# Hash attention and a PReLU block on one core: opening copies shared with VectorE, w_out's sums one step earlier, another way out for the last two blocks

## The chip, the cores and the metric

The kernel runs on one core of a Trainium2 chip. Its time is the device time of one execution in microseconds, as the median of several runs; smaller is better. Names of engines in the views: PE is TensorE (PEld its weight loads), DVE VectorE, ACT ScalarE, POOL GpSimd, SP SyncE, which here only issues DMAs.

## What is computed

The reference, cut to what matters:

```python
# attention: batch 4, heads 8, sequence 768, head size 64; proj is 64 x 6
q_bits = einsum(q, proj) > 0;  k_bits = einsum(k, proj) > 0     # 6 bits each
mask = bucket(q_bits) == bucket(k_bits)
scores = where(mask, (q @ k.T) / sqrt(64), -1e9)
attn = softmax(scores) @ v
x = attn as (3072 tokens, 512)
# feed-forward: w_in 512 x 2048, w_out 2048 x 512, alpha 2048
h = x @ w_in
g = maximum(h, 0) + alpha * minimum(h, 0)
out = g @ w_out
```

The two weights arrive as 64-bit floats; the kernel makes 32-bit floats of them on the core itself, and both weight products are done with seven instead of eight block products (Strassen), which needs sums of blocks of x, w_in, g and w_out.

## The kernel before

**Two paths.** `fast_path` does all the work under the assumption that the magnitudes are moderate; its `verdict` writes a flag, and only if that flag is set does `general_path` run behind it. In the runs here the fast path is what is timed. Most instructions are recorded with `do`, which keeps each engine's order as it is written in the program. DMAs are not recorded with it, so a scheduler may place them otherwise on SP's and POOL's queues.

**Attention** goes over 16 pairs of heads, each in two units of 384 queries (u = 0 to 31). `load` fetches q, k and v of a pair. `turn` transposes q and k on PE into a score bank pair and copies them out (qT, kT). `hash_bits` multiplies both with proj and turns the signs into bits (qb, kb). `scores` makes, for each of six blocks of keys, the products of the bits and of q and k in one bank pair (`sc`), and ACT takes the exponential into `pt`. The row sums are added beside it: `add_first` (L748) adds blocks 0 and 1 on DVE and has POOL issue a DMA that adds block 2 into the same tile (accp, L749); `add_last` adds blocks 3 to 5 (accd); `add_total` (L757) adds both. `attend` (L767) multiplies with v into the bank `av`, `totals` (L779) sums accd over the keys on PE into the bank `sm`, and `divide` normalizes and writes x (L808), from where it is stored.

PSUM has eight banks: three pairs that go around under tag "sc" (scores, transposes, hash banks, the "a" banks of the products), one "av", one "sm". So attend(u + 1) may start only when x of unit u has read `av`, and a score block only when the third one before it in that pool has been read.

**Weights** are converted in 32 pieces beside attention, one for each unit: `weight_abs` (ACT), `weight_clamp`, `weight_parts` and `weight_sum` (DVE). Piece 0 and the abs and clamp of piece 1 lie before or in unit 0.

**Opening.** Half of pair 0 is turned and hashed with DVE's help (`turn(..., DVE)`, `hash_bits(..., DVE)`), the other half and pair 1 by ACT alone. With `engine` DVE, hash_bits has a bank of its own for q's hashes (hsq, in `sm`), so that ACT and DVE can read different banks.

**Feed-forward.** For each of four batches come eight blocks "1" (`ff1`, products f_0 to f_7) and seven blocks "2" (`ff2`, products z_1 to z_7, in the order 1, 2, 5, 6, 3, 7, 4); j counts all blocks. `Product.step` issues parts of a product on PE: it uses the banks a (a pair of "sc"), b (`sm`) and c (`av`); `keep` copies a bank to SBUF with ACT, and `finish` adds the four quarters (named 11, 12, 21, 22) on DVE. In ff2, `finish` writes acc; for z_4 it adds the tile of z_1 (m1) too.

w_out's sums are formed once, in blocks j = 1 to 6 of the first batch: `load_out(n)` reads part n of eight on POOL's queue into the tile wo (two parts a tile, tag "wl", two buffers), `sum_out(n)` does four adds on DVE (L944) and stores the part on POOL's queue (L945). From j = 6 on `load_w2` loads whole w_out tiles on SP's queue (L928) into the same two buffers of tag "wl"; the first takes the memory of wo4 (parts 4 and 5), the second that of wo6 (parts 6 and 7), so each waits until those parts are stored. `largest` and `verdict` stand at j = 4.

**Output.** Results leave by `turn_out`: DVE transposes and twelve small DMAs on SP's queue (L1016). The last two blocks use `turn_last` (PE transposes, ACT copies at L1037, DMAs at L1038): block o_5 first, before the last part of z_4; then block o_4, which is z_4 itself. The tile of o_5 has tag "o" (two buffers, shared with turn_out), that of o_4 tag "m5" (one buffer).

Of the kernel before, what the change touches and what calls it, by code (L numbers as in the profile page):

```python
# [8 lines left out]
F32 = mybir.dt.float32  # L9
# [397 lines left out]
def fast_path(  # L407
# [165 lines left out]

    def weight_abs(i):
        i = order[i]
        lo, hi = halves(i)
        wx[i] = pool.tile([P, 512], F32, name=f"wx{i}", tag="wx")
        do(ACT.activation(wx[i], hi.bitcast(F32), AF.Abs))  # L580

    def weight_clamp(i):
# [105 lines left out]
    def hash_bits(pi, halves=BOTH, engine=None):  # L688

        if halves.start == 0:
            bits["q", pi] = qbs[pi % 2]
            bits["k", pi] = pool.tile([P, S], BF16, name=f"kb{pi}", tag="kb")
        ps = {"k": two_banks(f"hs{pi}")}
        ps["q"] = psum.tile([P, 1, 512], F32, name=f"hsq{pi}", tag="sm") if engine is DVE else ps["k"]
        for half in range(halves.start, halves.stop):
            for n, name in enumerate("kq"):
                for s in range(2):
                    r, c = D * s, D * (s ^ half) + 32 * n  # L700

                    for t, c in [("k", c)] + ([("q", c ^ D)] if engine is DVE and name == "q" else []):
                        do(PE.matmul(
                            ps[t][c : c + 32, half, :CW], wh[r : r + D],
                            tr[name, pi][r : r + D, half * CW : (half + 1) * CW], start=True, stop=True,
                        ))
        for half in range(halves.start, halves.stop):
            cols = slice(half * CW, (half + 1) * CW)
            for s in range(2):
                c = D * (s ^ half ^ (engine is DVE)) + 32  # L710
                do(ACT.activation(  # L711
                    bits["q", pi][D * s : D * s + 32, cols], ps["q"][c : c + 32, half, :CW], AF.Sign, bias=hb[c : c + 32],
                ))

            for to, c, n in [(0, 0, P)] if half == 0 else [(0, D, D), (D, 0, D)]:
                dst, src = bits["k", pi][to : to + n, cols], ps["k"][c : c + n, half, :CW]
                if engine is DVE:
                    do(DVE.tensor_scalar(
                        dst, src, hb_k[c : c + n, 0:1], hb_k[c : c + n, 1:2], op0=ALU.is_gt, op1=ALU.subtract,
                    ))  # L720
                else:
                    do(ACT.activation(dst, src, AF.Sign, bias=hb[c : c + n]))  # L722
# [112 lines left out]
    class Product:  # L835

        def __init__(self, name, width, nk, left, right, finish):
            self.name, self.width, self.nk = name, width, nk  # L840
            self.left, self.right, self.finish = left, right, finish
            self.ps, self.sb = {}, {}

# [20 lines left out]
        def step(self, n):  # L864
            if n == 1:
                self.times("a", 0, 0, True)
                self.keep("a", "p1")
            elif n == 2:
                self.times("b", 1, 1, True)
            elif n == 22:  # L870
                self.finish("11", self.sb["p1"], self.ps["b"])
            elif n == 5:
                self.times("c", 3, 3, True)
                self.keep("c", "p5")
            elif n == 6:
                self.times("a", 4, 4, False)
                self.keep("a", "u1")
            elif n == 3:
# [91 lines left out]
    def ff2(b, n):  # L970
# [11 lines left out]
        def finish(c, x, more):  # L982
            i, jj = int(c[0]) - 1, int(c[1]) - 1
            dst = acc[:, i, jj * HC : (jj + 1) * HC]
            if more is not None:
                do(DVE.tensor_tensor(dst, x, more, op=ALU.add))
                if p == 4:
                    add(4, 1, i, jj)
            elif p == 4:
                do(DVE.tensor_tensor(dst, x, m2[b, 1][:, i, jj * HC : (jj + 1) * HC], op=ALU.add))  # L990
            else:
                do(ACT.copy(dst, x))
            if c == "21":

                for to, x in {2: [(2, 1)], 6: [(1, 6)], 3: [(3, 5), (3, 1)], 7: [(1, 7), (5, 1)]}.get(p, []):
                    add(to, x)
                done = {2: (2, 0, 0), 3: (3, 0, 1), 7: (5, 1, 1), 4: (4, 1, 0)}.get(p)
                if done:
                    to_turn.append((b, *done))

        return Product(
            f"z{b}_{p}", HC, HK, lambda m, k: w2[b, n, m][:, k], lambda m, k: g2[b, n, m][:, k], finish,
        )

    def turn_out():
# [14 lines left out]

    def turn_last(n):

        b, p, half, ch = to_turn.pop(0)
        o = late[0].tile([P, CH, P, 2], F32, name=f"o_{p}", tag=("o", "m5")[n], bufs=2 - n)
        dst = out_v[b, ch * CH : (ch + 1) * CH].rearrange("c p d -> p c d")[:, :, half * 2 * P : (half + 1) * 2 * P]
        goes = [([(t, i) for i in range(2) for t in range(CH)], slice(0, CH))]
        if n:
            goes = [([(2, 0), (2, 1), (0, 0), (1, 0)], slice(2, CH)), ([(0, 1), (1, 1)], slice(0, 2))]
        for cells, ts in goes:
            ps = two_banks(f"to{p}").rearrange("p a f -> p (a f)").rearrange("p (i t f) -> p i t f", i=2, f=P)  # L1030
            for t, i in cells:
                do(PE.transpose(ps[:, i, t], m2[b, p][:, i, t * P : (t + 1) * P], ident))
            for i in range(2):
                t = [c[0] for c in cells if c[1] == i]
                if t:
                    t = slice(min(t), max(t) + 1)
                    do(ACT.copy(o[:, t, :, i], ps[:, i, t]))  # L1037
            (nc.scalar if n else nc.sync).dma_start(dst[:, ts], o[:, ts].rearrange("p t f i -> p t (f i)"))  # L1038


    top = const.tile([P, 4], F32, name="top")
    row = const.tile([1, 4], F32, name="row")

    def largest():
        do(DVE.tensor_reduce(top[:, :2], mags, axis=mybir.AxisListType.X, op=ALU.max))
        do(DVE.tensor_reduce(top[:, 2:3], wmax, axis=mybir.AxisListType.X, op=ALU.max))
        do(DVE.tensor_reduce(top[:, 3:4], alpha, axis=mybir.AxisListType.X, op=ALU.max))

    def verdict():
        ps = psum.tile([1, 4, P], F32, name="vd", tag="sm")  # L1050
        for n in range(4):
            do(PE.transpose(ps[:, n], top[:, n : n + 1], ident))
        do(DVE.tensor_reduce(row, ps, axis=mybir.AxisListType.X, op=ALU.max))
        do(DVE.tensor_tensor(row[:, 0:1], row[:, 0:1], row[:, 1:2], op=ALU.mult))

        do(DVE.tensor_scalar(row[:, 0:1], row[:, 0:1], SAFE, None, op0=ALU.is_le))
        do(DVE.tensor_scalar(row[:, 2:3], row[:, 2:3], HI_END, None, op0=ALU.is_lt))
        do(DVE.tensor_scalar(row[:, 3:4], row[:, 3:4], 1.0, None, op0=ALU.is_le))
        do(DVE.tensor_tensor(row[:, 0:1], row[:, 0:1], row[:, 2:3], op=ALU.mult))
        do(DVE.tensor_tensor(row[:, 0:1], row[:, 0:1], row[:, 3:4], op=ALU.mult))  # L1060
        do(DVE.tensor_scalar(flag, row[:, 0:1], -1.0, 1.0, op0=ALU.mult, op1=ALU.add))

# [36 lines left out]
    for u in range(UNITS):  # L1099
        pi, g = divmod(u, NCH)  # L1100

# [7 lines left out]
            scores(u + 1, 0)  # L1109
        if u:  # L1110
            divide(u - 1, weight_rest)
        else:
            weight_clamp(1)
        load_weight(u + 3)
        add_last(u)
        add_total(u)
        if u < last:
            add_first(u + 1)
        else:
            now = ff1(0, 0)  # L1120
            now.step(1)
# [41 lines left out]
    for j, (b, what, n) in enumerate(blocks):  # L1163
# [86 lines left out]
```

## Time and profile before

| | us |
|---|---|
| median of 3 runs | 902.18 (902.04 to 905.09) |
| the profiled execution | 901.85 |
| its span | 900.1 |
| mean granted TensorE clock | 0.997 |

| stage (us from the span's start) | PE busy | DVE busy | ACT busy |
|---|---|---|---|
| 0 to 25 | 21.70 | 13.02 | 18.05 |
| 25 to 50 | 25.00 | 21.27 | 21.30 |
| 50 to 400 | 350.00 | 309.69 | 262.04 |
| 420 to 430 | 8.30 | 9.83 | 1.59 |
| 500 to 700 | 200.00 | 158.97 | 46.06 |
| 890 to 895 | 2.35 | 1.75 | 1.96 |

The page gives busy time and waits of each engine. A row of a timeline has the start, the length, the engine, the line in the kernel, the operation, the tiles out<-in with their shape, and how often it stands there in a row; in brackets is how long the engine was idle before it and what ended that. A row of the waits has the total, the number and the longest wait. In the chain of work that ended last, each piece is one that the next had to wait for. A DMA's row on SP, ACT or POOL is its issue; the time from issue to landing is given by the DMA view.

### The profile page before, as it was taken

The numbers are of one execution on the slowest core, as the hardware profiler recorded it, in microseconds if no ns is written. First come the engines' busy times: TensorE is split into PE (matmuls) and PEld (weight loads), VectorE is DVE, ScalarE is ACT, GpSimd is POOL, SyncE is SP. The second block draws the span as 40 slices with busy tenths as digits, with TensorE's granted clock in tenths as the row PEclk, the third lists the DMA queues.
The fourth block names the chain that finished last, engine by engine and source line by source line (L and its number), as shares of the span: only waits on it lengthen the run. The fifth ranks groups of instructions, "written<-read, shape, count | busy, mean of one in ns | idle before, by whom it ended". The sixth has DMA issues, their size and how long they took to land.

```text
span 900.1 us, 15656 instructions
## 1 busy us (share of the span) xinstructions
PE 887.3 (99%) x5885; PEld 591.3 (66%) x5885; DVE 754.5 (84%) x1353; ACT 408.6 (45%) x733; POOL 100.4 (11%) x194
## 2 busy tenths in 40 slices
PE   8999999999999999999999999999999999999996
PEld 4444445444444445556997557997557998556996
DVE  4888988988999996899889668988668989768985
ACT  6888888887888863222112222112222111222111
POOL 1222222222232222110000000000000000000000
PEclk9999999999999999999999999999999999999998
DMA  9788998699798665477343525243526242530242
GB/s 238 162 199 181 204 227 213 170 266 276 171 235 210 182 159 178 174 257 289 138 140 88 181 88 188 98 154 83 172 98 193 94 158 76 161 114 0 95 153 62
DMA packets 131909, 146.88 MB, mean 163 GB/s; under 512 B 78304, under 2 KB 118000, under 8 KB 128240
## 3 DMA queue, kind: packets, MB, share of 16 engines
q1 hardware_dynamic: 118800, 124.03, 44.7%
q0 software_dynamic: 11008, 20.97, 11.8%
q8 instruction: 48, 0.79, 0.4%
q10 hardware_dynamic: 2016, 0.79, 0.3%
q14 instruction: 37, 0.30, 0.1%
HBM read 104.87 MB, written 28.31 MB: 148 GB/s over the span
## 4 chain that ended last, share of the span: by engine, by line
PE 92%; issue 3%; DMA 3%; ACT 1%; POOL 1%; DVE 0%; ACTq 0%; POOLq 0%; SPq 0%
PE sc L734 17%; PE av L767 14%; PE z_2a L854 2%; PE f_0a L854 2%; PE z_4a L854 2%; PE z_7a L854 2%; PE z_3a L854 2%; PE z_6a L854 2%; PE z_5a L854 2%; PE f_1a L854 2%; PE f_2a L854 2%; DMA w_out_s<-wo 2%; PE z_1a L854 2%; PE f_7a L854 2%; PE f_6a L854 2%
## 5 line engine op out<-in xcount | busy, mean ns | idle before, releaser
L739 ACT ACTIVATE pt<-sc 128x768 f32<-128x768 f32 x192 | 152.8, 813 | 46.7 <-PE sc L734 44.4
L734 PE MATMUL sc<-qT,kT 64*128 64x384 f32 x768 | 155.3, 482 | 0.0
L767 PE MATMUL av<-pt,vn 128*32 128x384 f32 (+1 forms) x1536 | 130.6, 488 | 0.0
L767 PEld LDWEIGHTS av<-pt,vn 128*32 128x32 f32 x1536 | 46.6, 109 | 75.1 <-issue 71.5
L734 PEld LDWEIGHTS sc<-qT,kT 64*128 64x128 f32 x768 | 68.2, 188 | 35.1 <-issue 34.8
L904 DVE TENSOR_TENSOR g<-g,g 128x384 f32<-128x384 f32 x128 | 68.4, 555 | 2.2
L734 PE MATMUL sc<-qb,kb 64*128 64x384 bf16 x384 | 63.4, 324 | 1.9 <-ACT kb L722 1.0
L749 POOL DMA_DIRECT2D accp<-pt x32 | 38.6, 1205 | 193.3 <-issue 73.0
L968 DVE TENSOR_TENSOR gs<-g,gs 128x768 f32<-128x768 f32 x56 | 53.4, 953 | 1.0
L960 DVE TENSOR_TENSOR ws<-wl 128x512 f32<-128x512 f32 x56 | 38.5, 688 | 18.5 <-DMA wl<-w_out_s 16.2
L968 DVE TENSOR_TENSOR gs<-g 128x768 f32<-128x768 f32 x56 | 53.3, 953 | 0.0
L900 DVE SCALAR_TENSOR_TENSOR g<-h,alpha 128x384 f32<-128x384 f32 x32 | 19.7, 617 | 26.0 <-ACT h L893 26.0
L734 PEld LDWEIGHTS <-kb 64*128 64x128 bf16 x384 | 19.4, 94 | 33.2 <-issue 11.1
L757 DVE TENSOR_TENSOR accd<-accd,accp 128x768 f32<-128x768 f32 x32 | 30.7, 958 | 6.5 <-DMA accp<-pt 5.5
L711 ACT ACTIVATE qb<-hs,hb 32x384 bf16<-32x384 f32 x62 | 35.5, 573 | 1.1
L754 DVE TENSOR_TENSOR accd<-accd,pt 128x768 f32<-128x768 f32 x32 | 30.7, 959 | 3.3
L748 DVE TENSOR_TENSOR accp<-pt,pt 128x768 f32<-128x768 f32 x32 | 30.5, 952 | 2.7 <-ACT pt L739 2.7
L753 DVE TENSOR_TENSOR accd<-pt,pt 128x768 f32<-128x768 f32 x32 | 30.4, 949 | 0.0
L803 POOL COPY rr<-rr 32x6 f32<-32x6 f32 x64 | 27.6, 431 | 2.6
L980 DVE TENSOR_TENSOR m<-m,m 128x768 f32<-128x768 f32 (+1 forms) x36 | 27.1, 752 | 0.7
L722 ACT ACTIVATE kb<-hs,hb 64x384 bf16<-64x384 f32 (+1 forms) x47 | 27.1, 577 | 0.6
L802 POOL COPY rr<-rr 32x6 f32<-32x6 f32 x64 | 19.8, 310 | 63.2 <-DVE rr L799 61.9
(336 smaller groups left out, 1807.4 us busy)
## 6 DMA issues: line engine op xcount, KB each, us to landing
wi<-w_in_s SPq DMA_DIRECT2D x32, 896.0 KB, 4.8
wl<-w_out_s SPq DMA_DIRECT2D x16, 1024.0 KB, 4.8
accp<-pt POOLq DMA_DIRECT2D x32, 384.0 KB, 5.2
wl<-w_out_r SPq DMA_DIRECT2D x12, 1024.0 KB, 4.8
raw<-in_moe_w_out_dram SPq DMA_DIRECT2D x16, 512.0 KB, 5.3
raw<-in_moe_w_in_dram SPq DMA_DIRECT2D x16, 512.0 KB, 5.3
w_in_s<-wsi SPq DMA_DIRECT2D x16, 448.0 KB, 5.8
vn<-in_v_dram SPq DMA_DIRECT2D x16, 384.0 KB, 6.1
```

The costliest lines, as they stand in the source:

```text
L711: do(ACT.activation(bits["q", pi][D * s : D * s + 32, cols], ps["q"][c : c + 32, half, :CW], AF.Sign, bias=hb[c : c + 32],))
L734: do(PE.matmul(sc[:, s, :CW], what["k", pi][r, ks], what["q", pi][r, qs], start=first, stop=not first,))
L739: do(ACT.activation(pt[:, :, :CW], sc[:, :, :CW], AF.Exp, scale=SCALE / DOWN))
L748: do(DVE.tensor_tensor(accp[u], p(u, 0), p(u, 1), op=ALU.add))
L749: nc.gpsimd.dma_start(accp[u], p(u, 2), accum_op=ALU.add)
L754: do(DVE.tensor_tensor(accd[u], accd[u], p(u, 5), op=ALU.add))
L757: do(DVE.tensor_tensor(accd[u], accd[u], accp[u], op=ALU.add))
L767: do(PE.matmul(av[u][D * s + t : D * s + t + 32, :w], nat["v", pi][:, s, kc * D + t : kc * D + t + 32], prob[u, kc][:, s, :w], start=(kc = ...
L854: do(PE.matmul(self.ps[bank], self.left(left, k), self.right(right, k), start=start and k == 0, stop=k == self.nk - 1, skip_group_check=no ...
L904: do(DVE.tensor_tensor(new_g(b, to)[:, i], g_m[b, x][:, i], g_m[b, y][:, i], op=ALU.subtract))
L960: do(DVE.tensor_tensor(t, w2[b, n, x], w2[b, n, y], op=op))
L968: do(DVE.tensor_tensor(t, g2[b, n, x], g2[b, n, y], op=ALU.subtract))
```

## The change

1. **Opening.** The second half of pair 0 is hashed with DVE (`hash_bits(0, second, DVE)`), and kT of pair 1 is copied by DVE. Both turns of pair 1 come ahead of `add_first(0)` on the engines that do both. In the form with DVE, q is hashed ahead of k. The abs of pieces 0 and 1 moves from ACT to DVE, as a bitwise and. The abs and clamp of piece 1 move from before unit 0's totals to behind `add_first(1)`, that is, behind unit 0's total.
2. **w_out's sums.** Part 3 is loaded and summed one block earlier (j = 3 instead of 4), part 6 too (j = 5 instead of 6).
3. **Verdict.** One transpose of a 128 x 4 tile takes the place of four of 128 x 1; the maxima then go through a 32 x 32 transpose on DVE.
4. **z_4.** A hook `kept` adds m1 to a quarter as soon as its first summand is in SBUF, ahead of the second summand; the number of adds stays.
5. **End.** The block o_5 is copied from two single banks and goes out on ACT's queue. The block o_4 is split in three: two pieces (tx, tz) are copied by DVE into one tile that now has tag "o", one (ty) by ACT into a tile with tag "m5"; ty's DMA is on ACT's queue, the last one on SP's.

```diff
-    def weight_abs(i):
+    def weight_abs(i, engine=None):
...
+        if engine is DVE:
+            do(DVE.tensor_scalar(wx[i].bitcast(U32), hi, 0x7FFFFFFF, None, op0=ALU.bitwise_and))
+            return
         do(ACT.activation(wx[i], hi.bitcast(F32), AF.Abs))
...
-            for n, name in enumerate("kq"):
+            for name in "qk" if engine is DVE else "kq":
...
     def turn_last(n):
...
+        def cells(name, at):
+            ps = two_banks(f"{name}{p}")[:, 0].rearrange("p (t f) -> p t f", f=P)
+            for k, (t, i) in enumerate(at):
+                do(PE.transpose(ps[:, k], m2[b, p][:, i, t * P : (t + 1) * P], ident))
+            return ps[:, : len(at)]
+
+        if n == 0:
+            o = late[0].tile([P, CH, P, 2], F32, name=f"o_{p}", tag="o")
             for i in range(2):
+                do(ACT.copy(o[:, :, :, i], cells(f"to{i}", [(t, i) for t in range(CH)])))
+
+            nc.scalar.dma_start(dst, o.rearrange("p t f i -> p t (f i)"))
+            return
+        o = late[0].tile([P, 2, P, 2], F32, name=f"o_{p}", tag="o")
+        o2 = late[0].tile([P, P, 2], F32, name=f"o2_{p}", tag="m5", bufs=1)
+        ps = cells("tx", [(0, 0), (1, 0)])
+        ps2 = cells("ty", [(2, 0), (2, 1)])
+        do(DVE.tensor_copy(o[:, :, :, 0], ps))
+        do(ACT.copy(o2.rearrange("p f i -> p i f"), ps2))
+        nc.scalar.dma_start(dst[:, 2], o2.rearrange("p f i -> p (f i)"))
+        do(DVE.tensor_copy(o[:, :, :, 1], cells("tz", [(0, 1), (1, 1)])))
+        nc.sync.dma_start(dst[:, :2], o.rearrange("p t f i -> p t (f i)"))
...
     def verdict():
-        ps = psum.tile([1, 4, P], F32, name="vd", tag="sm")
-        for n in range(4):
-            do(PE.transpose(ps[:, n], top[:, n : n + 1], ident))
-        do(DVE.tensor_reduce(row, ps, axis=mybir.AxisListType.X, op=ALU.max))
+        ps = psum.tile([4, P], F32, name="vd", tag="sm")
+        do(PE.transpose(ps, top, ident))
+        do(DVE.tensor_reduce(col[:4, 0:1], ps, axis=mybir.AxisListType.X, op=ALU.max))
+        do(DVE.transpose(row, col))
...
     scores(0, 0)
+    hash_bits(0, second, DVE)
+    turn(1, "q")
+    turn(1, "k", BOTH, DVE)
     add_first(0)
-    hash_bits(0, second)
-    weight_abs(0)
+
+    weight_abs(0, DVE)
     weight_clamp(0)
     weight_parts(0)
     weight_sum(0)
-    for name in "qk":
-        turn(1, name)
-    weight_abs(1)
...
         if u:
             divide(u - 1, weight_rest)
-        else:
-            weight_clamp(1)
...
         if u < last:
             add_first(u + 1)
+            if u == 0:
+                weight_abs(1, DVE)
+                weight_clamp(1)
...
-        for n_out in [(), (0,), (1,), (2,), (3, 4), (5,), (6, 7)][j] if j < 7 else ():
+        for n_out in [(), (0,), (1,), (2, 3), (4,), (5, 6), (7,)][j] if j < 7 else ():
             sum_out(n_out)
-        for n_out in [(1,), (2,), (3,), (4, 5), (6, 7)][j] if j < 5 else ():
+        for n_out in [(1,), (2, 3), (4,), (5, 6), (7,)][j] if j < 5 else ():
             load_out(n_out)
```

More of the change, by code (lines that the diff above doesn't have):

```diff
@@ L697, in hash_bits @@
         for half in range(halves.start, halves.stop):
-            for n, name in enumerate("kq"):
+            for name in "qk" if engine is DVE else "kq":
                 for s in range(2):
-                    r, c = D * s, D * (s ^ half) + 32 * n
+                    r, c = D * s, D * (s ^ half) + 32 * "kq".index(name)
                     for t, c in [("k", c)] + ([("q", c ^ D)] if engine is DVE and name == "q" else []):
                         do(PE.matmul(
-                            ps[t][c : c + 32, half, :CW], wh[r : r + D],
+                            ps[t][c : c + 32, half if t == "k" or engine is not DVE else 0, :CW], wh[r : r + D],
                             tr[name, pi][r : r + D, half * CW : (half + 1) * CW], start=True, stop=True,
@@ L711, in hash_bits @@
                 do(ACT.activation(
-                    bits["q", pi][D * s : D * s + 32, cols], ps["q"][c : c + 32, half, :CW], AF.Sign, bias=hb[c : c + 32],
+                    bits["q", pi][D * s : D * s + 32, cols], ps["q"][c : c + 32, 0 if engine is DVE else half, :CW], AF.Sign, bias=hb[c : c + 32],
                 ))
@@ L835, in fast_path, with __init__ @@
     class Product:
-        def __init__(self, name, width, nk, left, right, finish):
+        def __init__(self, name, width, nk, left, right, finish, kept=None):
             self.name, self.width, self.nk = name, width, nk
+            self.kept = kept if kept else lambda c, t: None
             self.left, self.right, self.finish = left, right, finish
@@ L870, in step @@
             elif n == 22:
+                self.kept("11", self.sb["p1"])
                 self.finish("11", self.sb["p1"], self.ps["b"])
@@ L877, in step @@
                 self.keep("a", "u1")
+                self.kept("22", self.sb["p5"])
+                self.kept("12", self.sb["u1"])
             elif n == 3:
@@ L984, in finish @@
             dst = acc[:, i, jj * HC : (jj + 1) * HC]
-            if more is not None:
+            if p == 4:
+                do(DVE.tensor_tensor(dst, m2[b, 1][:, i, jj * HC : (jj + 1) * HC] if more is None else dst, x if more is None else more, op=ALU.add))
+            elif more is not None:
                 do(DVE.tensor_tensor(dst, x, more, op=ALU.add))
[L987 to L990, printed above, removed]
             else:
@@ L999, in finish, with kept @@
                     to_turn.append((b, *done))
+        def kept(c, x):
+            i, jj = int(c[0]) - 1, int(c[1]) - 1
+            m = m2[b, 1][:, i, jj * HC : (jj + 1) * HC]
+            do(DVE.tensor_tensor(acc[:, i, jj * HC : (jj + 1) * HC], x, m, op=ALU.add))
         return Product(
             f"z{b}_{p}", HC, HK, lambda m, k: w2[b, n, m][:, k], lambda m, k: g2[b, n, m][:, k], finish,
+            kept if p == 4 else None,
         )
@@ L1023, in turn_last @@
         b, p, half, ch = to_turn.pop(0)
-        o = late[0].tile([P, CH, P, 2], F32, name=f"o_{p}", tag=("o", "m5")[n], bufs=2 - n)
         dst = out_v[b, ch * CH : (ch + 1) * CH].rearrange("c p d -> p c d")[:, :, half * 2 * P : (half + 1) * 2 * P]
[L1026 to L1032, printed above, removed]
-            for i in range(2):
[L1034 to L1038, printed above, removed]
+        def cells(name, at):
[3 more added lines that the diff above has]
+            return ps[:, : len(at)]
@@ L1041, in fast_path @@
+        ps2 = cells("ty", [(2, 0), (2, 1)])
[4 more added lines that the diff above has]
+        nc.sync.dma_start(dst[:, :2], o.rearrange("p t f i -> p t (f i)"))
     top = const.tile([P, 4], F32, name="top")
-    row = const.tile([1, 4], F32, name="row")
+    col = const.tile([32, 32], F32, name="col")
@@ L1044, in largest @@
+    row = const.tile([32, 32], F32, name="row")
     def largest():
+        do(DVE.memset(col, 0.0))
         do(DVE.tensor_reduce(top[:, :2], mags, axis=mybir.AxisListType.X, op=ALU.max))
@@ L1049, in verdict @@
     def verdict():
-        ps = psum.tile([1, 4, P], F32, name="vd", tag="sm")
-        for n in range(4):
-            do(PE.transpose(ps[:, n], top[:, n : n + 1], ident))
-        do(DVE.tensor_reduce(row, ps, axis=mybir.AxisListType.X, op=ALU.max))
[L1054 to L1061, printed above, removed]
+        ps = psum.tile([4, P], F32, name="vd", tag="sm")
+        do(PE.transpose(ps, top, ident))
+        do(DVE.tensor_reduce(col[:4, 0:1], ps, axis=mybir.AxisListType.X, op=ALU.max))
+        do(DVE.transpose(row, col))
+        do(DVE.tensor_tensor(row[0:1, 0:1], row[0:1, 0:1], row[0:1, 1:2], op=ALU.mult))
+        do(DVE.tensor_scalar(row[0:1, 0:1], row[0:1, 0:1], SAFE, None, op0=ALU.is_le))
+        do(DVE.tensor_scalar(row[0:1, 2:3], row[0:1, 2:3], HI_END, None, op0=ALU.is_lt))
+        do(DVE.tensor_scalar(row[0:1, 3:4], row[0:1, 3:4], 1.0, None, op0=ALU.is_le))
+        do(DVE.tensor_tensor(row[0:1, 0:1], row[0:1, 0:1], row[0:1, 2:3], op=ALU.mult))
+        do(DVE.tensor_tensor(row[0:1, 0:1], row[0:1, 0:1], row[0:1, 3:4], op=ALU.mult))
+        do(DVE.tensor_scalar(flag, row[0:1, 0:1], -1.0, 1.0, op0=ALU.mult, op1=ALU.add))
     last = UNITS - 1
```

## The prediction

> **What bounds it now.** I read the busy shares first, then the waits of TensorE (PE), then the order of time where those waits lie, then the chain around the last of them, then the end.
>
> ```profile
> span 900.1 us, 15656 instructions
> PE 887.3 (99%) x5885; PEld 591.3 (66%) x5885; DVE 754.5 (84%) x1353; ACT 408.6 (45%) x733; POOL 100.4 (11%) x194
> ```
> PE is busy 99% of the span. No row of PE is taken away except three transposes of the verdict, so the change can win only idle time of PE, 12.8 us: 3.3 in the first 25 us (stages view, 21.70 busy), 1.7 near 425 us, and 7.7 behind the last transpose (892.4 to 900.1).
>
> ```profile
> PE z_2a L854 <- DMA wl<-w_out_r: 1.7, 1, 1.7
> PE sc L734 <- ACT kb L722: 1.0, 1, 1.0
> PE sc L734 <- ACT qT L680: 0.4, 1, 0.4
> ```
> From 30 us to the end PE waits once, for the second w_out tile. The other waits lie in the opening:
>
> ```profile
> 13.31 1.36 POOL L749 DMA_DIRECT2D accp<-pt  x1 [10.34 <-DVE accp L748]
> 13.68 1.18 ACT L722 ACTIVATE kb<-hs,hb 64x384 bf16<-64x384 f32 x2
> 14.88 0.67 ACT L580 ACTIVATE wx<-raw 128x512 f32<-128x512 f32 x1
> 14.91 0.34 PE L734 MATMUL sc<-qb,kb 64*128 64x384 bf16 x2 [1.03 <-ACT kb L722]
> 16.14 0.80 ACT L680 ACTIVATE kT<-tp_k 128x768 f32<-128x768 f32 x1
> 20.79 0.51 PE L703 MATMUL hs<-kT,wh 64*32 64x384 f32 x2
> 21.95 0.96 DVE L757 TENSOR_TENSOR accd<-accd,accp 128x768 f32<-128x768 f32 x1
> ...
> 29.34 0.62 DVE L808 SCALAR_TENSOR_TENSOR x<-av,vs,dn 128x384 f32<-128x384 f32 x1
> 32.35 4.08 PE L767 MATMUL av<-pt,vn 128*32 128x384 f32 x48
> ```
> ACT is full from 10.06 to 21.7 us and PE waits for its copies. VectorE (DVE) is late there too: x of unit 0 (ends 29.96) must have read the only av bank before attend(1) may start at 32.35, a slack of 2.4 us.
>
> ```profile
> 411.92 9.63 DMA w_out_s<-wo
> ...
> 421.62 4.80 DMA wl<-w_out_r
> ...
> 426.46 1.58 PE z_2a L854 x8
> ```
> The second w_out tile waits for the memory of wo6, until that tile's last sums are stored.
>
> ```profile
> 886.85 5.56 SPq L1016 DMA_DIRECT2D out_dram<-o  x12
> 891.46 0.36 DVE L990 TENSOR_TENSOR m<-z_4a,m 128x192 f32<-128x192 f32 x1
> 892.51 0.40 SPq L1038 DMA_DIRECT2D out_dram<-o  x1
> 893.66 0.39 ACTq L1038 DMA_DIRECT2D out_dram<-o  x1
> ```
> At the end the last 256 KB go out at 893.66 and land 3.9 us later (DMA view), at 897.56.
>
> **Opening, PE's side.** Kept out of ACT before unit 1: two kb halves (1.18), kT (0.80), two abs (0.67 each), 3.3 us. With q hashed first, qb no longer waits for kT. From 8.47, when the first score block can start, PE has nine blocks of 0.81, one hash of 0.85 and two turns of 0.77: 9.7 us, so the hash of pair 1 could start at 18.15 instead of 20.79. I checked the three score banks in turn: kb done on DVE at 13.05, qT on ACT at 13.8, kT on DVE at 14.3; each comes before its block. Gain up to there 2.6 us.
>
> **Opening, DVE's side.** What ACT loses stands now on DVE ahead of add_first(0): kb 2 x 0.6, kT 0.96 (0.56 for half of it at L678). accp of unit 0 ends at 15.25 instead of 12.67, and its accumulating DMA is issued 0.6 later (as before: 12.67 to 13.31), at 15.85. That transfer has taken 7.8 us here, beside the loads that fill the DMA engines to 22 us, and 4.4 for unit 1 when they were idle (9.6 at the longest in the run). It starts later but the loads are the same, so I take 6.6: it lands at 22.45. DVE itself would be at that sum at 15.25 + abs 0.45 + clamp, parts and sum 3.7 (15.58 to 19.29) + two sums 2.0 = 21.4, so DVE waits a microsecond, and the total ends at 23.4. Behind it now stand accp 0.95, the second abs 0.45 and clamp 0.70 (moved from before the totals), parts 1.6, then vs to x, 4.05 (25.75 to 29.96 less a wait of 0.17): 7.75 us. x ends at 31.2. PE would be at attend(1) at 23.4 + 6.85 = 30.3 (25.50 to 32.35 before), so it waits 0.9 for x. Gain left at attend(1): 32.35 - 31.2 = 1.15. Bounds: landing after 4.4 us, 2.25; after 7.8, zero. From attend(1) on DVE needs 9.6 us to the next x and PE 10.25, so it holds.
>
> One rule bears on it. No row shows the abs on DVE; it reads every second word. The trace's nearest strided row is L597, 0.69, its contiguous one L593, 0.43. The Trainium skill (VectorE: DVE Perf Modes, "What auto-detection actually checks") gives two elements a cycle to a one-source op with source and destination in SBUF and even outer sizes, and does not ask for unit stride; L597 has two sources. By the rule 0.43, by the row 0.69, 0.25 us later at x. I take 0.43.
>
> **Sums of w_out.** Number 3 goes from j = 4 to 3, number 6 from j = 6 to 5; 0.44 per add, 1.75 per number. At j = 3 this makes DVE late by 1.75: top, done at 386.22, is done at 388.03 with the new memset. PE comes to the verdict at 387.51 and waits 0.5; it then has one transpose for four (0.44 from 387.51 to 387.95, now 0.15). The next product starts at about 388.2 instead of 387.95: a loss of 0.25, bounds -0.3 (no wait) and +0.6 (hash-bank "sm" still being read when f_5b comes; the reduce over 128 instead of 512 ends 0.2 ahead of it). After that DVE's idle gaps before f_4u and f_4p (0.28 and 0.57), the shorter reduce (0.67 to about 0.25, plus a 32x32 transpose of about 0.2) and number 3's adds, which no longer stand at j = 4, put DVE about a microsecond ahead; j = 5 adds 1.75 and j = 6 takes it off. The last sum ends near 410.7 instead of 411.6, and number 6 has been stored 7 us earlier. So the last store goes out at 410.8, with half a megabyte less beside it and one x load moved behind the tile's load on SP's queue. About 1.7 MB at 0.37 MB/us are left to move: it lands near 416.5, the tile near 421.5, and PE needs it at 424.76. Gain 1.7; if all cover fails, 0.8 (only the 0.9 us of earlier issue). DVE, 98% busy there, is 0.9 us earlier, so it doesn't take the place of the wait. POOL's queue is passed by these stores and loads alone, its waits (4.6 and 1.9 us) keep nobody.
>
> **Other blocks.** In z_4 the m1 adds come first; six adds of 0.35 remain six. Nothing gained: before, the last add started 891.46 just as the product ended (891.43).
>
> **End.** Block o_5 (384 KB) goes to ACT's queue at 891.05 instead of 892.51 behind SP's twelve. The last block's six transposes now start after the last add (the first of its banks is z_4a's), end near 892.7, and DVE could copy tz by 893.15. But its tile has moved from tag "m5" to tag "o", and in the changed program it has the memory of o_5: its first copy waits until o_5's DMA has landed. By the row, 4.1 us for that block, that is 895.15. The Trainium skill (DMA: Bandwidth & Descriptors, "Issuing engines are not separate DMA queues") says that transfers of all issuing engines run on the same 16 DMA engines and interleave; so the block no longer shares with the other two, only with SP's last three of 32 KB: 1.6 (one of those) + 384 KB at 330 GB/s, 1.2 = 2.8, that is 893.85. I take 894.2. Two copies of 0.42 follow, SP issues at 895.05, and 256 KB alone need 1.6 + 0.8 to 2.9: landing 897.45 to 897.95 against 897.56. Loss 0.15, bounds -0.5 and +0.8.
>
> **Sum.** -1.15 + 0.25 - 1.7 + 0.15 = -2.45. The profiled execution took 901.85, 0.33 below the median of 902.18; off the median, 899.7.
>
> **Rivals.**
> - All covers hold (0.16): accp lands after 4.4 us, no verdict wait, the end gains 0.5: -2.25 - 0.3 - 1.7 - 0.5 = -4.75, 897.4. For it: PE alone could do it; against: the loads are queued before accp.
> - The tile's wait stays, because the store is slowed by the four other transfers of those microseconds (it took 9.6 us, against 3.4 at best): -0.75, 901.4 (0.17).
> - Slower (0.15): DVE becomes the bound of the opening. If accp takes 9.6 us, as the longest one did, it lands at 25.45 and x ends at 34.2, 1.85 later than before: +1.85 + 0.25 - 1.7 + 0.15 = +0.55, 902.7. It decides from a landing of 9.05 us on.
>
> The forecast has 0.52. A measurement here tells 0.5%, 4.5 us, from no change: 897.67 and 906.7 are the limits. Faster than that is about two thirds of the first rival, 0.10; slower 0.03; the rest 0.87. Range 897.4 to 902.5: from the first rival's sum to just under the slower one.
>
> **What would show it.** The hash of pair 1 at 18.2; DVE waiting for accp's landing near 22.4; PE waiting about 0.9 for x before the second av; a wait of 0.5 at the verdict; no wait before z_2a; the tx copy idle until o_5 has landed, and the last DMA near 895 less the gains. Wrong if PE's hash of pair 1 is still near 20, if accp lands by 20, or if the copy of tx follows its transposes at once.

## The result and the profile after

| | before | after |
|---|---|---|
| median of 6 runs | 902.19 (901.37 to 905.09) | 899.57 (899.25 to 901.41) |
| the profiled execution | 901.85 | 899.33 |
| its span | 900.1 | 897.5 |

The ratio is 0.9969, with a 95% interval of 0.9954 to 0.9984: 2.8 us less, and between 1.4 and 4.2. The forecast was 899.7.

The page of the kernel after: PE's idle time has gone from 12.8 to 11.1 us (span less busy).

```profile
span 897.5 us, 15668 instructions
PE 886.4 (99%) x5886; PEld 590.7 (66%) x5886; DVE 757.3 (84%) x1362; ACT 406.2 (45%) x726; POOL 100.4 (11%) x194
```

Its waits of PE (total, times, longest). The tile's DMA and ACT's copies are gone; but for the first row, which was there before, each new row names DVE:

```profile
PE nil L516 <- DVE hb L520: 1.2, 1, 1.2
PE sm L782 <- DVE accd L760: 0.9, 1, 0.9
PE z_2c L858 <- DVE m L996: 0.7, 1, 0.7
PE av L770 <- DVE x L811: 0.5, 1, 0.5
PE vd L1075 <- DVE top L1071: 0.3, 1, 0.3
```

The same places in the timeline after:

```profile
15.24 0.42 DVE L581 TENSOR_SCALAR wx<-raw 128x512 uint32<-128x512 uint32 x1
15.96 1.36 POOL L752 DMA_DIRECT2D accp<-pt  x1 [12.99 <-DVE wx L581]
18.47 0.51 PE L706 MATMUL hs<-kT,wh 64*32 64x384 f32 x2
23.21 0.96 DVE L760 TENSOR_TENSOR accd<-accd,accp 128x768 f32<-128x768 f32 x1 [1.53 <-DMA accp<-pt]
31.04 0.62 DVE L811 SCALAR_TENSOR_TENSOR x<-av,vs,dn 128x384 f32<-128x384 f32 x1
31.71 4.08 PE L770 MATMUL av<-pt,vn 128*32 128x384 f32 x48 [0.55 <-DVE x L811]
...
387.35 0.27 PE L1075 MATMUL vd<-ident,top 128*4 128x128 f32 x1 [0.32 <-DVE top L1071]
410.13 0.75 POOL L952 DMA_DIRECT2D w_out_s<-wo  x1 [6.45 <-DVE wo L951]
417.56 0.32 SPq L935 DMA_DIRECT2D wl<-w_out_r  x1
423.64 1.46 PE L858 MATMUL z_2a<-g,wl 128*128 128x192 f32 x8
426.24 1.46 PE L858 MATMUL z_2b<-g,wl 128*128 128x192 f32 x8
428.41 1.57 PE L858 MATMUL z_2c<-gs,ws 128*128 128x192 f32 x8 [0.71 <-DVE m L996]
...
888.69 0.45 ACTq L1050 DMA_DIRECT2D out_dram<-o  x1
891.79 0.42 DVE L1056 COPY o<-tx 128x256 f32<-128x256 f32 x1 [2.04 <-DMA out_dram<-o]
892.57 0.39 SPq L1060 DMA_DIRECT2D out_dram<-o  x1
```

Read against the rows of before: the hash of pair 1 starts 2.3 us earlier (20.79 to 18.47), but attend(1) only 0.64 earlier (32.35 to 31.71). The second w_out tile is asked for 4.1 earlier (421.62 to 417.56) and no longer waited for; two products later PE waits for DVE instead. The copy of tx is idle for 2 us until a store has landed.

### The profile page after: what moved, and what is told of

The parts are those of the page before. It is cut to its first block, busy times and chain, and to the rows that moved or that the text cites. A ratio compares the mean times of both kernels' runs of the same rounds, so it can differ in the third digit from the quotient of the medians.

```text
span 897.5 us, 15668 instructions
## 1 busy us (share of the span) xinstructions
PE 886.4 (99%) x5886; PEld 590.7 (66%) x5886; DVE 757.3 (84%) x1362; ACT 406.2 (45%) x726; POOL 100.4 (11%) x194
## 4 chain that ended last, share of the span: by engine, by line
PE 89%; DVE 7%; DMA 2%; issue 1%; SPq 1%; ACT 0%; DVEq 0%; ACTq 0%
PE sc L737 17%; PE av L770 14%; PE f_0a L858 2%; PE z_3a L858 2%; PE z_6a L858 2%; PE z_5a L858 2%; PE f_2a L858 2%; PE f_1a L858 2%; PE z_2a L858 2%; PE f_3a L858 2%; PE z_7a L858 2%; PE z_1a L858 2%; PE z_4a L858 2%; PE f_7a L858 2%; PE f_6a L858 2%; PE f_5a L858 2%
## 5 line engine op out<-in xcount | busy, mean ns | idle before, releaser
L800 DVE STREAM_TRANSPOSE st<-sm 128x192 f32<-128x192 f32 x32 | 12.2, 381 | 14.0 <-PE sm L782 13.8
```

## A ruler: the span in five stages

PE runs through most of the kernel without a gap, so the starts of five of its rows cut a trace into stages: the totals of unit 17 (sm), attend(30) (av), f_5a, the last part of z_4a, and the span's end. This table is worked out from the rows of all fourteen traces; "to attend(1)" lies within the first stage.

| trace | to attend(1) | 0 to sm 17 | to av 30 | to f_5a | to z_4a | to the end |
|---|---|---|---|---|---|---|
| before | 32.35 | 203.16 | 128.98 | 55.81 | 501.93 | 10.22 |
| e1 opening alone | 31.81 | 202.61 | 130.00 | 55.80 | 504.15 | 10.04 |
| e2 sums alone | 32.07 | 202.87 | 128.99 | 56.10 | 500.30 | 9.84 |
| e3 end alone | 32.16 | 202.96 | 128.99 | 55.80 | 501.98 | 10.07 |
| e4 verdict alone | 32.04 | 202.84 | 129.87 | 55.47 | 502.49 | 9.93 |
| after | 31.71 | 202.52 | 128.99 | 55.95 | 500.36 | 9.68 |
| e10 after, old opening | 31.80 | 202.60 | 129.50 | 55.96 | 500.36 | 10.18 |
| e5 own tile | 31.65 | 202.45 | 128.99 | 55.94 | 500.29 | 9.53 |
| e6 third add on DVE | 31.27 | 202.08 | 129.85 | 55.95 | 501.10 | 9.82 |
| e7 abs on ACT | 31.29 | 202.09 | 128.99 | 55.94 | 500.30 | 10.38 |
| e8 sums earlier | 31.37 | 202.18 | 128.99 | 55.47 | 499.37 | 9.89 |
| e9 all four | 30.75 | 201.55 | 128.99 | 55.47 | 499.43 | 9.26 |
| e11 last store on ACT | 30.48 | 201.28 | 128.99 | 55.48 | 499.42 | 9.63 |
| e12 loads moved | 30.21 | 201.01 | 128.99 | 55.47 | 499.43 | 9.30 |

The verdict's stage repeats to 0.02 us. The middle is 128.99 or up to 1.0 more, in code that no edit touched. For one form of the code the opening scatters by 0.4 to 0.6, the end by 0.4 to 0.7. So stages tell what the times (scatter of 1 to 3 us) cannot, where the difference is larger than that or comes in several traces.

## Experiments

**One part alone on the kernel before (e1 to e4).** e1 has the opening's part of the diff, e2 only this:

```diff
-        for n_out in [(), (0,), (1,), (2,), (3, 4), (5,), (6, 7)][j] if j < 7 else ():
+        for n_out in [(), (0,), (1,), (2, 3), (4,), (5, 6), (7,)][j] if j < 7 else ():
-        for n_out in [(1,), (2,), (3,), (4, 5), (6, 7)][j] if j < 5 else ():
+        for n_out in [(1,), (2, 3), (4,), (5, 6), (7,)][j] if j < 5 else ():
```

> The kernel before with the opening alone changed (keys' bits, kT and the first two weights' magnitudes on VectorE, q hashed first, the second piece behind the first total). Theory: ACT is relieved by 2.3 us at the hash of pair 1 (18.5 instead of 20.8), but VectorE gives most of it back: it waits about 1.5 us for accp's landing before the first total, and x of unit 0 ends after PE wants to start attend(1). Left at attend(1): 0.64 us (31.7 instead of 32.35), and 0.6 us of the whole time, 901.6. First rival: the relief of ACT is kept in full, 2.3 us, 899.9. Second rival: the later waits of the kernel (the second w_out tile, which depends on VectorE's order and not on PE's) swallow it, 0, 902.2.

Measured: 902.58 against 902.38 for before, ratio 0.9994 (0.9979 to 1.001). attend(1) is 0.54 earlier than in the trace of before, so ACT's full 2.3 us is out. But in the median of all twelve runs nothing of it reaches the end, as the second rival has it. In this trace the accumulating DMA is late in mid-attention, PE waits for x twice there, and the wait for the tile grows from 1.7 to 2.4. Its timeline, then its waits of PE:

```profile
211.69 0.96 DVE L760 TENSOR_TENSOR accd<-accd,accp 128x768 f32<-128x768 f32 x1 [2.70 <-DMA accp<-pt]
222.48 0.96 DVE L760 TENSOR_TENSOR accd<-accd,accp 128x768 f32<-128x768 f32 x1 [1.66 <-DMA accp<-pt]
230.28 4.09 PE L770 MATMUL av<-pt,vn 128*32 128x385 f32 x48 [0.50 <-DVE x L811]
251.50 4.09 PE L770 MATMUL av<-pt,vn 128*32 128x385 f32 x48 [0.30 <-DVE x L811]
...
427.61 2.50 PE L857 MATMUL z_2a<-g,wl 128*128 128x192 f32 x8 [2.41 <-DMA wl<-w_out_r]
```
```profile
PE z_2a L857 <- DMA wl<-w_out_r: 2.4, 1, 2.4
PE sm L782 <- DVE accd L760: 1.7, 1, 1.7
PE av L770 <- DVE x L811: 1.3, 3, 0.5
```

Something else lengthens this execution. Behind that wait PE's granted clock falls. A row of the stages view has the stretch, its length, the busy time of PE, PEld, DVE, ACT and POOL, then the granted clock, the DMA share and the GB/s:

```profile
428.00:432.00 4.00, 4.00 (x16) 4.00 (x15) 3.93 (x8) 0.32 (x1) 0.00 (x0) 0.57 0.54 213
```

In quarters of a microsecond the clock is 0.50 from 428.25 to 431.5. From z_2a to z_2c PE takes 5.69 us, against 4.02 in before: 1.67 are lost on top of the wait. Up to the last product no other of the fourteen traces has such a stretch; e4's wait of 2.27 left the clock at 1.00. The mean clock of e1's execution is 0.996. Among the runs of the versions that wait for the tile (before, e1, e3, e4), 30 of 99 have a mean of 0.996 or less; among those that don't (e2, after, e5 to e12), none of 72. So the lowered clock goes with this wait. That every low mean is such a stretch is argued from one trace.

It splits e1's twelve runs: six at 0.996 or less have a median of 904.3, the six others 900.6, where the 24 such runs of before beside them have 902.0. So the opening alone does win time where the clock holds, and more than the 0.54 at attend(1); where the rest comes from is open. Whether it makes the lowered clock commoner (6 of 12 against 11 of 35) is open.

> The kernel before with the two lists of sum_out and load_out alone changed. Theory: wl_1 is issued about 4 us earlier (417.5 instead of 421.6), PE doesn't wait for the tile at z_2a any more (1.7 us before), and a wait for VectorE at z_2c of up to 0.7 us takes part of its place; before that the verdict costs PE up to 0.5 us, because VectorE reaches the four maxima 1.75 us later, and this part isn't lost in the wait for the tile, since that wait is gone. Sum -0.6 to -1.3, about 901.1. First rival: the tile's wait goes and nothing takes its place, -1.7 or better, 900.5. Second rival: the transfer is only hidden elsewhere, the 0.9 us of earlier issue alone are won and the verdict takes 0.5 of them, -0.4, 901.8.

Measured: 900.66 against 902.38, ratio 0.998 (0.9965 to 0.9994). By stages +0.29 at the verdict and -1.63 in the products: -1.34, at the strong edge of the theory, and as much as against the runs of before with an unlowered clock (902.0). The time alone would fit the first rival too; the trace decides. Both ends of the exchange are there: no wait for the tile, and at z_2c, in the waits of PE:

```profile
PE z_2c L854 <- DVE m L986: 0.6, 1, 0.6
```

> The kernel before with the new turn_last alone (two copiers, three small groups of transposes, the bigger block on ACT's queue; z_4's adds as before). Theory: the 384 KB block leaves 2 to 2.5 us earlier, the copies of the last block are held up by its landing since both tiles have the same memory, and the end of the span comes 0.3 to 0.7 us earlier relative to the last product: -0.5, 901.7. Rival: the shared memory costs as much as the copies and the queue win, 0 to +0.5, 902.2 to 902.7. If the shared memory didn't matter the last store would go out at 891.5 instead of 893.7 and the time would be 2 us less, 900.2.

Measured: 902.28 against 902.38, ratio 0.9999 (0.9989 to 1.0008). The theory's 0.5 falls; the rival holds. The copy of tx waits 1.91 for the store of o_5; SP's store of 256 KB goes out at 894.37, 0.7 later than in the trace of before, and lands after 3.2 instead of 3.9.

> The kernel before with the one-transpose verdict alone. VectorE has the four maxima here 1.3 us before PE comes to the verdict, so PE doesn't wait for them; it saves three transposes, 0.29 us. Theory: this gain is swallowed at z_2a, where PE waits for the w_out tile whose time depends on VectorE's adds; VectorE itself gains 0.4 on the reduce and loses 0.3 on memset and turn. So 0 to -0.2, 902.1. Rival: the 0.29 us of PE are kept, 901.9; a loss would show that the short operations on one partition cost VectorE more than the reduce of 4 x 128 on one.

Measured: 903.04 against 902.38, ratio 1.0011 (1.0001 to 1.002). The verdict's stage is 0.34 shorter, three transposes as expected. The trace is longer all the same, 0.9 in mid-attention (DVE waits 2.75 for accp at 211.98, and PE 0.7 for x behind it) and 0.56 in the products, where PE waits 2.3 for the tile. The 0.9 lies in a place that the edit doesn't reach. The 0.56 is at least in part what the theory said: PE comes 0.34 earlier to a tile that does not come earlier. Six of the twelve runs have a mean clock of 0.996 or less (median 903.8), but the six others (902.6) are no faster than before. Whether slow executions are commoner with the edit (the interval just excludes 1) or fell to it by chance is open.

**The old opening in the kernel after (e10)**, the first hunks of the diff undone.

> The kernel after with the opening of the kernel before; sums, verdict and end stay. It asks what the opening is worth where the wait for the w_out tile at z_2a is gone. Theory: 0.64 us at attend(1), and all of it arrives at the end, as VectorE's order in the products follows PE's: 900.2. First rival: the relief of ACT counts in full, 2.3: 901.9. Second rival: z_2c's wait for VectorE absorbs it: 899.6.

Measured: 900.77, ratio to before 0.9975 (0.9963 to 0.9987), against 0.9969 for the kernel after. 2.3 us is out; between 0 and 0.64 the times don't decide. The traces do it together: with the old opening (before, e2, e3, e4, e10) attend(1) starts at 32.08 on average, with the new one (after, e1, e5, e8) at 31.64. It is worth 0.45, give or take 0.3, since each form scatters (31.80 to 32.35 and 31.37 to 31.81).

**What holds the opening (e6, e7), on the kernel after.** e6:

```diff
-        nc.gpsimd.dma_start(accp[u], p(u, 2), accum_op=ALU.add)
+        if u:
+            nc.gpsimd.dma_start(accp[u], p(u, 2), accum_op=ALU.add)
...
         do(DVE.tensor_tensor(accd[u], accd[u], p(u, 5), op=ALU.add))
+        if not u:
+            do(DVE.tensor_tensor(accp[u], accp[u], p(u, 2), op=ALU.add))
```

> The kernel after, where for unit 0 alone the third summand of accp is added on VectorE (0.96 us more there) and the accumulating DMA of 384 KB is left away. Theory: VectorE's wait of 1.5 us for that DMA goes, the first total starts 0.6 us earlier (22.6 instead of 23.21), so sm of unit 0 0.6 us earlier and x of unit 0 too, and attend(1) starts 0.5 to 0.6 earlier: 899.0. Rival: it is VectorE's work and not the landing that sets the opening, then the 0.96 us more on it are lost: +0.4 to +0.9, 900.2.

Measured: 898.69, ratio to before 0.9956 (0.9942 to 0.9971). Timeline of e6:

```profile
21.59 0.95 DVE L760 TENSOR_TENSOR accp<-accp,pt 128x768 f32<-128x768 f32 x1
22.57 0.96 DVE L763 TENSOR_TENSOR accd<-accd,accp 128x768 f32<-128x768 f32 x1
23.58 0.53 PE L785 MATMUL sm<-accd,ones 128*32 128x192 f32 x8
31.27 1.18 PE L773 MATMUL av<-pt,vn 128*32 128x384 f32 x12 [0.75 <-DVE x L814]
```

DVE does 0.96 us more and is at the first total 0.64 earlier: the landing held it. Counted from the hash of pair 1 the total starts 3.85 us behind in e6, e9, e11 and e12, which don't have this DMA, and 4.74 to 5.56 in the five traces that do. attend(1) is 0.44 earlier; now DVE's chain to x is the limit, with 0.75 of wait. e7 shortens that chain:

```diff
-                weight_abs(1, DVE)
+                weight_abs(1)
```

> The kernel after, with the magnitude of the second weight piece back on ACT. Theory: between the first total and x of unit 0 VectorE is never idle, so x ends 0.45 us earlier and PE's wait of 0.55 us before attend(1) shrinks to 0.1; sm of unit 0 stays where it is, provided that ACT's 0.67 us for it fall behind its exponentials of unit 0: -0.4, 899.15. Rival: ACT hasn't the time, a score block waits for it, and the gain is taken back: 0 to +0.3, 899.7.

Measured: 899.31, ratio 0.9962 (0.9948 to 0.9977). attend(1) is 0.42 earlier and has no wait for x; timeline of e7:

```profile
31.29 3.11 PE L770 MATMUL av<-pt,vn 128*32 128x384 f32 x36
```

sm stays at 24.26, held by accp (1.3 of wait). e8, with the opening of after, has attend(1) at 31.37, so that start alone would not decide. The distance from the first total does: 8.50 or 8.51 in the four traces with the opening of after, 8.05 in e7. So two limits follow one another: the landing sets the first total, DVE's work behind it sets x. Together they add up (e9: 30.75, 0.96 earlier).

**The sums once more earlier (e8)**, on the kernel after:

```diff
-        for n_out in [(), (0,), (1,), (2, 3), (4,), (5, 6), (7,)][j] if j < 7 else ():
+        for n_out in [(), (0, 1), (2, 3), (4,), (5, 6), (7,), ()][j] if j < 7 else ():
-        for n_out in [(1,), (2, 3), (4,), (5, 6), (7,)][j] if j < 5 else ():
+        for n_out in [(1, 2, 3), (4, 5), (6, 7), (), ()][j] if j < 5 else ():
```

> The kernel after, with each sum of w_out behind the first one step earlier still (number 1 at j = 1, 2 and 3 at j = 2, 4 at j = 3, 5 and 6 at j = 4, 7 at j = 5) and the loads with them. Theory: VectorE's lag of 0.7 us at z_2c comes from the adds of the last w_out sums, and goes, since they stand 10 us earlier; the verdict's wait of 0.3 us may go too (one number at j = 3 instead of two) or shift to another place at j = 4: -0.4 to -0.9, 899.0. Rival: VectorE is full in all these blocks (98% busy), and the lag only moves to an earlier product: 0 to +0.5, 899.8.

Measured: 897.55, ratio 0.9947 (0.9932 to 0.9963). Both waits are gone, 0.48 at the verdict and 0.99 in the products, more than expected. All waits of PE that are left:

```profile
PE nil L516 <- DVE hb L520: 1.2, 1, 1.2
PE sm L782 <- DVE accd L760: 1.1, 1, 1.1
PE av L770 <- DVE x L811: 0.6, 1, 0.6
```

**The end (e5, e11).** e5 gives the last block a tile of its own:

```diff
-        o = late[0].tile([P, 2, P, 2], F32, name=f"o_{p}", tag="o")
+        o = late[0].tile([P, 2, P, 2], F32, name=f"o_{p}", tag="m1", bufs=1)
```

> The kernel after, with o of the last block in memory of its own (the free tile m1 instead of o), so that its copies don't wait for the landing of the block before. Theory: VectorE's copy of tx starts right behind tx and the last sum (about 889.8 instead of 891.79), the last store of 256 KB goes out near 890.9 instead of 892.57, and since it then shares the DMA engines with the 384 KB sent at 888.7, it lands 0.3 to 0.9 us slower than alone: -0.8 to -1.5, about 898.3. Rival: the transfers are the limit, 640 KB that must leave behind the last product, and nothing is won: 899.5.

Measured: 898.83, ratio 0.9954 (0.994 to 0.9969). The copies follow their transposes at once, but the store doesn't follow the copies; timeline and SP's waits of e5:

```profile
889.71 0.42 DVE L1056 COPY o<-tx 128x256 f32<-128x256 f32 x1
890.14 0.42 DVE L1059 COPY o<-tz 128x256 f32<-128x256 f32 x1
891.74 0.39 SPq L1060 DMA_DIRECT2D out_dram<-o  x1
```
```profile
SPq L1060 <- DMA out_dram<-o: 2.1, 1, 2.1
```

A second coupling stood behind the first: the store goes out just as the 384 KB store lands (888.55 + 3.1 = 891.65; in e9 886.31 + 3.1, and it goes out at 889.42), though it has memory of its own. In the built program, as the expectation of e11 says, it waits for the DMA semaphore that the 384 KB store counts on. The theory got 0.8 of the 1.7 us that it expected for the store. Its gain shows in several traces: the last stage takes 9.26 to 9.63 in the four with the own tile and 9.68 to 10.38 in the six without it, 0.6 less on average. e11 keeps the four edits of e9 and sends it from ACT's queue:

```diff
-        nc.sync.dma_start(dst[:, :2], o.rearrange("p t f i -> p t (f i)"))
+        nc.scalar.dma_start(dst[:, :2], o.rearrange("p t f i -> p t (f i)"))
```

> All four edits, and the last store of 256 KB on ACT's queue instead of SP's. In the run with the tile of its own, VectorE's copies were done at 890.56, but SP issued that store at 891.74 only; in the built program it waits for the same DMA semaphore that the 384 KB store counts on, so for that store's landing (888.55 + 3.1). On ACT's queue the program gives it another semaphore. Theory: the store goes out 0.1 to 0.3 us behind its copies instead of 1.2, lands with the 384 KB store still under way, and the span ends 0.6 to 1.0 us earlier than with the four edits: 895.2. Rival: the transfers themselves set the end (768 KB behind the last product), and it lands no earlier: 896.0.

Measured: 896.84 against 896.59 for e9. The store goes out as its copies end, and nothing is won. Timeline and DMA view of e11 (size, median from issue to landing):

```profile
887.64 0.42 DVE L1062 COPY o<-tz 128x256 f32<-128x256 f32 x1
888.10 0.38 ACTq L1063 DMA_DIRECT2D out_dram<-o  x1
```
```profile
out_dram<-o ACTq DMA_DIRECT2D x1, 384.0 KB, 2.6
out_dram<-o ACTq DMA_DIRECT2D x1, 256.0 KB, 4.2
```

Issued 1.1 earlier against the last transpose than in e9, it takes 4.2 instead of 3.0. The landing counted from the start of the last z_4a is 7.13 (888.10 + 4.2 - 885.17) against 6.98 (889.42 + 3.0 - 885.44): the rival holds, here the transfers are the limit.

**All four edits (e9)**: e5, e6, e7 and e8 together.

> The kernel after with four edits at once: tile of its own for the last block, third summand of unit 0 on VectorE, second magnitude on ACT, w_out sums one step earlier. Theory: behind the opening PE waits for nothing with the earlier sums, so what the opening wins (0.6 and 0.45 us at attend(1)) is carried to the end and adds up with the 1.6 us of the earlier sums and 0.3 to 0.8 of the end: 896.0, span near 894.2. Rival: the gains overlap, since VectorE sets the pace in the product blocks: 897.5, as with the earlier sums alone.

Measured: 896.59 (before beside it 902.61), ratio 0.9933 (0.9916 to 0.995). The profiled span is 894.7, 2.8 below that of after: -0.97 opening, -0.48 verdict, -0.93 products, -0.42 end. The gains add up. The rival's 897.5 lies above the measured time, if within its interval; it is the stages that decide. This version is faster than both kernels.

**Where executions differ (e12)**: as e11, with load_w(0) to load_w(2) put behind units 24, 26 and 28 in the program.

> As the kernel with the last store on ACT's queue, and the loads of the first three w_in tiles (load_w 0 to 2) moved from units 18 and 25 to units 24, 26 and 28; x's loads stay at unit 18. It asks where the spread between executions comes from: near 211 us VectorE waits 2.3 to 2.8 us for an accumulating DMA in every trace, and in three of ten traces PE then waits 0.6 to 0.8 us in all for x near 230 to 251 us. Theory: the loads at unit 18 crowd that DMA; the wait at 211 falls under 1.5 us, PE doesn't wait for x in the middle, and the median comes 0.2 to 0.6 us nearer to the fastest run: 894.9. Rival: other traffic of these units (the keys', queries' and x's) does it, the wait stays, 895.2.

Measured: 896.46. Inconclusive: the edit moved nothing. SP issued those loads as early as before, since nothing that they need comes later; the timeline of e12 (in e11 the row starts at 190.77), and the wait it was to remove:

```profile
190.53 7.40 SPq L839 DMA_DIRECT2D wi<-w_in_s  x3
209.91 0.96 DVE L763 TENSOR_TENSOR accd<-accd,accp 128x768 f32<-128x768 f32 x1 [2.52 <-DMA accp<-pt]
```

## Why the prediction was right, step by step

| step | predicted | the one profile | traces together |
|---|---|---|---|
| opening, at attend(1) | -1.15 | -0.64 | -0.45 |
| verdict | +0.25 | +0.14 | +0.14 |
| w_out's sums | -1.7 | -1.57 | -1.6 |
| end | +0.15 | -0.54 | 0.0 |
| sum | -2.45 | -2.6 | -1.9 |

For the sums the last column takes the traces whose middle wasn't late; with e1 and e4, where the wait was longer and e1's clock fell, it would be -2.2.

- **Opening, the mechanism right, the landing mis-sized.** ACT's relief came as worked out (2.3 of the 2.6). DVE waits for accp and PE for x, as foretold. The term that was off is the 6.6 us for the accumulating DMA: the total that waits for it starts at 23.21 instead of 22.45, 7.25 behind the issue. The chain behind it took 0.3 less than the 7.75 worked out, so x ends at 31.66 instead of 31.2. Both limits were real, as e6 and e7 show. The other 0.2 between -0.64 and -0.45 is scatter: the opening of before was the latest of its form.
- **The abs by the rule or the row.** 0.42 us: the rule of the perf modes held, the strided row with two sources was no guide.
- **Verdict.** By the spacing of starts PE waits 0.48 (vd stands 1.77 behind the product part before it, 1.29 in before), as worked out; the row of the waits lists 0.3. One transpose instead of four gives 0.33 back (the next product stands 0.11 behind vd instead of 0.44). Alone, the sums cost 0.29 (e2) and the new verdict saved 0.34 (e4); together they lose 0.14. The one transpose needs all the maxima, while in e2 the first of four starts at 387.52, before the last maximum is done at 387.64.
- **w_out.** Two errors cancelled, which is luck. Up to z_2a the gain was not the 1.7 of the wait's row but 2.33 by the spacing of starts (z_2a behind f_5a: 38.51 before, 36.18 after). In before the tile itself cost 1.86, 3.16 from z_1a to z_2a where after has 1.30:

```profile
423.30 1.46 PE L854 MATMUL z_1a<-gs,ws 128*128 128x192 f32 x8
426.46 1.58 PE L854 MATMUL z_2a<-g,wl 128*128 128x192 f32 x8 [1.70 <-DMA wl<-w_out_r]
```

The other 0.47 are four small delays just ahead of it (from z_1b on, parts of the product 1.38 to 1.48 apart instead of 1.30), which stand in no row of the waits and are gone after. The prediction has no term for them. And the step "DVE, 98% busy there, is 0.9 us earlier, so it doesn't take the place of the wait" failed: z_2c stands 2.17 behind z_2b where e8 has 1.30, so DVE took back 0.87. The chain of waits after runs through DVE there without PE from 400 to 428:

```profile
422.15 1.04 DVE g L911 x2
423.21 0.56 DVE g L911
423.77 0.87 DVE gs L975
424.64 0.26 DVE m L996
...
428.01 0.36 DVE m L996
428.37 0.04 issue
428.41 1.57 PE z_2c L858 x8
```

- **End.** The wait of tx for the store of o_5 came as foretold, and that store took 2.9 where 2.8 was worked out from engines that all queues share; e11, where another queue won nothing, fits that too. The last store lands 7.4 to 8.1 us behind the start of the last z_4a in the six traces with this end, 7.4 to 7.7 in the four with the old one (7.7 and 7.5 on average). So the sum of +0.15 was about right, and the -0.54 of the one pair of profiles is scatter.
- **z_4.** Nothing gained, as foretold: the last add starts 1.58 behind the start of the last z_4a in before and after (891.46 and 889.40). It was not run alone.
- **The whole.** The traces account for 1.9 us, the pair of profiles for 2.6, since the execution of before had the latest opening of five and the longest end of four. The times (1.4 to 4.2) agree with both. They hold one thing that the forecast has no term for: 16 of the 63 runs of before that stand beside the experiments have a mean clock of 0.996 or less and a median of 904.2, the others 902.1, and with the tile's wait these executions go. That the forecast of 899.7 lies 0.1 from the measured median is therefore luck in part. The first rival, all covers hold (897.4), and the slower one (902.7) lie outside what was measured; nor did the tile's wait stay (901.4).

## What to carry over

Compare the spacing of starts between two traces, not only the rows of the waits: the wait for the tile was listed as 1.7 and cost 1.86, and 0.47 more stood ahead of it in no row. Look at the granted clock behind a long wait: in e1 it cost 1.67 us more than the wait itself. Work that is moved earlier on a nearly full engine (DVE's adds) pays only as far as that engine's next due date allows; look for the product that is due next and move the work past it too (e8 won 1.5 more). Where a store is held up, look for all that couples it to the one before (memory, semaphore, the transfer engines), and cost the last of these before spending effort on the first.

## What the runs showed of the hardware

- PE's granted clock can fall behind a wait. In e1, after 2.41 us without a matmul, it was 0.50 for some 3.4 us and three product parts took 5.69 us instead of 4.02; in e4, after 2.27, it stayed at 1.00. What decides between the two is not shown.
- The same accumulating DMA of 384 KB takes 4.4 us where less moves (226 to 242 us in after: 189 GB/s) and 9.9 where more does (196 to 212: 330 GB/s). It is behind DVE's wait of 2.3 to 2.8 us near 211 in every trace; in four of fourteen the middle then takes 0.5 to 1.0 longer. That this makes part of the spread between executions is likely, but e12 did not test it.
- A DVE operation of 0.43 us can take 0.68 beside POOL's issue of a DMA. L596 does in after at 16.42, inside the issue of 15.96 to 17.32; in e6, where POOL issues nothing then, it takes 0.43 at 16.67, but 0.68 at 25.49, inside an issue of 25.03 to 26.39. In the first 80 us of the fourteen traces nine rows of this form (L596 or L599) start 0.46 or 0.47 us behind the start of an issue, and all take 0.67 or 0.68; five that start 0.53 or 0.54 behind it take 0.47 or 0.48, four at 0 to 0.07 and all from 1.04 on 0.43. The Trainium skill (SBUF — State Buffer, "SBUF: two separate sides") says that VectorE in a two-port mode and GpSimd share a pair of ports, that whichever starts first holds it for its whole instruction, and that the other is blocked. A DVE operation that grows fits that in kind, but 0.25 us is less than the 0.90 that the issue of 1.36 still had to run, and no run here shows that it is this lock.
